# A gated linear recurrence and a maxout FFN: two time steps in each partition, and recurrence groups of one batch

## The chip, the cores and the metric

The kernel runs on one core of a Trainium2 chip. The metric is the device time of one execution in microseconds, taken as the median over runs. The profile is one further execution, recorded by the hardware profiler.

## The reference

Four inputs q, k, v and alpha have the shape (4 batches, 8 heads, 768 time steps, 48) in fp32. Each head carries a 48 by 48 state through time; the outputs of all heads, 384 values a token, go through a feed-forward network (FFN) with three parallel first layers of which the largest value is kept.

```python
for t in range(S):
    state = alpha[:, :, t, :, None] * state + einsum('bhd,bhe->bhde', k[:, :, t], v[:, :, t])
    y[:, :, t] = einsum('bhd,bhde->bhe', q[:, :, t], state)
x = y.transpose(0, 2, 1, 3).reshape(4 * 768, 384)
h = maximum(maximum(x @ w1, x @ w2), x @ w3)      # 768 wide
out = h @ w_out                                   # 3072 x 384
```

## The kernel before

**Tiles.** Time is cut into 6 blocks of 128 steps, with time on the partitions. One *unit* u is one block of one batch with all 8 heads; there are 24, block by block, with the batches inside a block. Two units are a *group* n: the same block of two batches. There are 12 groups, and a group is also what the FFN takes at a time (256 tokens).

**The recurrence, unit by unit.** `load` (L344) brings alpha, q, k and v of a group, 384 KB each in runs of 48 fp32 (192 bytes), into one of five sets of buffers. `decay` (L366) takes logarithms of alpha on ACT (L373), sums them over each half block on PE (L388, "totals") and makes from neighbouring blocks the factor G (L400). `prep` (L405) makes cumulative sums inside the block with one matmul against a triangular constant (L416), takes exponentials of them and of their negatives on ACT (L419, L421), multiplies q and k by them (L428, on POOL, or on DVE for the units listed in `EARLY`), scales v to fp16 (L439), transposes q and k on PE (L452, 16 transposes of 64 rows), copies them out of PSUM on DVE (L471), forms the scores k.q on PE (L480, 8 matmuls of 48 rows by 128 columns, of which two run on the two halves of the array's rows) and masks them on DVE (L485). `output` (L498) adds, in one PSUM bank, the part of the state (L509) and the part inside the block (L512), copies with a scale on ACT (L520), turns the result (L527) and copies it to xT on DVE (L531). `state` (L534) forms k.v over the block (L545), adds the old state on DVE (L551) and multiplies by G on POOL (L558); the state Z is kept in two copies that take turns.

**The FFN, group by group.** `ffn` (L567) has nine pieces of six matmuls (L582; three weights, two column tiles of 128, three row tiles). The piece of the first weight is copied by ACT (L590), those of the other two are joined by a maximum on DVE (L594). Then come twelve matmuls with w_out (L607), a copy on ACT (L615) and the store (L618).

**What sets the order.** Nothing is scheduled by hand: every piece of work is a step with an engine, a planned cost, a rank, what it reads and writes, and the PSUM banks it needs (eight in all). `Plan.order` runs a list schedule over all steps with these costs, and the instructions are then written out in that order, so each engine executes its own list strictly in turn. A step with `mode=1` uses half of PE's rows; the planner adds a cost for a change of mode, and from unit 6 on the scores of one unit and the transposes of the next are one step (`window`, L464). The loads and stores go through SP's queue (L350, L618), the four weights, cast to fp16 on the way, through POOL's queue (L362), each behind the k of a certain unit (`WAFTER`).

Of the kernel before, what the change touches and what calls it, by code (L numbers as in the profile page):

```python
# [18 lines left out]
CDEC = 0.92  # L19
# [4 lines left out]
TURN_RANK, TURN_COST = 2.0, 0.1  # L24
SP_FIRST = 0.9
QUEUES = ("SP", "POOL")
DMA_IN, DMA_OUT, DMA_SLOW = 0.9, 0.9, 1.0
DMA_BOTH = {"SP": 0.3, "POOL": 0.7}


class Transfers:
# [9 lines left out]
    def next(self, commit=False):  # L41
        now = self.now
        left = {e: [list(j) for j in js[:1]] for e, js in self.jobs.items()}
        while True:
# [8 lines left out]
            rate = DMA_BOTH if len(on) > 1 else dict.fromkeys(QUEUES, 1.0)  # L53
# [15 lines left out]
            return end, j[2]  # L69


class Plan:
# [55 lines left out]
    def order(self):  # L128
# [20 lines left out]
        free = dict(dict.fromkeys(HOP, 0.0), SP=SP_FIRST)  # L149
        bank_free = {b: 0.0 for b in range(NBANKS)}  # L150
        place, seq, recent = {}, [], []
# [18 lines left out]
        while len(seq) < n:  # L170
            best = None
            for e, cand in pending.items():
                pick = None
                for i in cand:
                    at = self.homes(bank_free, self.steps[i][5])
                    if at is None:
                        continue
                    t = max(ready[i], free[e], at[0])
                    turn = TURN_RANK if e == "PE" and self.steps[i][7] != mode else 0.0
                    key = (t, self.steps[i][2] + turn, i)  # L180
                    if pick is None or key < pick:
                        pick = key
                if pick is not None and (best is None or pick < best[0]):
                    best = (pick, e)
            landing = dma.next()
            if landing and (best is None or landing[0] + DMA_OUT <= best[0][0]):
                end, i = dma.next(commit=True)
                self.landed[i] = end + DMA_OUT
                finish(i, end + DMA_OUT)
                continue  # L190
# [17 lines left out]
            if load:  # L208
                dma.add(e, t + cost + DMA_IN, load, i)
            else:  # L210
                finish(i, t + cost + HOP[e])
# [7 lines left out]
def kernel(  # L219
# [38 lines left out]
    halves = np.stack([rr < HALF, rr >= HALF], axis=1).astype(np.float32)  # L258
    c16_np = np.concatenate(
        [trimid, np.eye(P), (s_ <= t_).astype(np.float32), halves], axis=1  # L260
    ).astype(np.float16)
    dec = CDEC ** (rr - (HALF - 1.0))
    c32_np = np.stack(
        [SIG / dec, dec / SIG, np.full(P, HALF * np.log(CDEC))], axis=1
# [5 lines left out]
    c16 = sb.tile([P, 3 * P + 2], FP16, name="c16")  # L270
    c32 = sb.tile([P, 3], FP32, name="c32")
    tri, ident = c16[:, :P], c16[:, P:2 * P]
    maskA, hsel = c16[:, 2 * P:3 * P], c16[:, 3 * P:]
# [9 lines left out]
    ld = {x: homes(5, [P, HG, D], FP32, x + "n") for x in "aqkv"}  # L283
    las = homes(3, [P, HG, DP], FP16, "la")
    eps = homes(3, [P, H, D], FP32, "ep")
    ens = homes(3, [P, H, D], FP32, "en")
    qks = homes(7, [P, 2, H, DP], FP16, "qk")
    v16s = homes(7, [P, H, D], FP16, "v")
    qkTs = homes(3, [P, 2, NP, P], FP16, "qkT")
    LAs = homes(3, [P, 2, NP, P], FP16, "LA")  # L290
# [4 lines left out]
    Us = homes(3, [P, NP, 2 * D], FP32, "U")  # L295
    Zs = [homes(B, [P, NP, 2 * D], FP16, f"Z{i}_") for i in range(2)]
    e12s = homes(4, [P, HG // 2, 2], FP32, "e")
    Gs = homes(3, [P, HG // 2], FP32, "G")
    wcat = sb.tile([P, NFT, 3, DF], FP16, name="wcat")
    wo16 = sb.tile([P, NJ, DM], FP16, name="wo16")  # L300
    zero = sb.tile([P, 2 * P], FP16, name="zero")
    nc.vector.memset(zero, 0.0)
    for t in las:
        nc.vector.memset(t[:, :, D:], 0.0)
    for t in qks:
        nc.vector.memset(t[:, :, :, D:], 0.0)
    for zz in Zs:
        for t in zz:
            nc.vector.memset(t, 0.0)

    plan = Plan({x: range(NBANKS) for x in ("Lp", "hp", "tp", "A", "yp", "xp", "pp", "gp", "op", "fill")})
# [13 lines left out]
    def banks2(key, dtype):  # L325
# [4 lines left out]
    LEAD = 6.5  # L330
    WAFTER = {2: (0,), 3: (1, 2), 5: (3,)}
    FILL = 0
    FUSED = 6
    pending = []
    TP = 0.24
    EARLY = {0: ("DVE", "POOL", "POOL"), 1: ("DVE", "DVE", "ACT"),
             3: ("DVE", "DVE", "ACT"), 6: ("DVE", "DVE", "POOL"),
             7: ("POOL", "POOL", "POOL")}


    views = {n: x.rearrange("b h s d -> s (b h) d") for n, x in
             (("a", alpha), ("q", q), ("k", k), ("v", v))}

    def load(n, lo, hi, names="aqkv"):  # L344
        cb, g = divmod(n, B // UB)
        for x in names:
            t = ld[x][n % 5]

            def run(x=x, t=t):
                nc.sync.dma_start(  # L350
                    t[:, lo:hi],
                    views[x][cb * P:(cb + 1) * P, g * HG + lo:g * HG + hi])

            plan.step("SP", 0.5, -1.0, run, line="loads",
                      writes=[(x, n % 5, h) for h in range(lo // H, hi // H)],
                      load=1.8 * (hi - lo) / HG)

    def weights(g, gate):
# [4 lines left out]
                  reads=[gate], writes=[("w", g)], line="weights", load=3.5)  # L363


    def decay(n):  # L366
        cb, g = divmod(n, B // UB)
        la, an = las[n % 3], ld["a"][n % 5]
        rank = 2 * n - 0.5

        def ln(lo, hi):
            plan.step("ACT", 0.11 + 0.00072 * (hi - lo) * D, rank,
                      lambda: nc.scalar.activation(out=la[:, lo:hi, :D], in_=an[:, lo:hi, :],  # L373
                                                   func=AFT.Ln, scale=1.0 / CDEC),
                      reads=[("a", n % 5, h) for h in range(lo // H, hi // H)],
                      writes=[("la", n % 3, h) for h in range(lo // H, hi // H)])

        if n == 0:
            ln(0, H)
            ln(H, HG)  # L380
        else:
            ln(0, HG)
        key = ("hp", n)

        def totals():
            live[key] = bank(key, [P, HG // 2, 2], FP32)
            for j in range(HG // 2):
                nc.tensor.matmul(live[key][:, j, :], la[:, 2 * j:2 * j + 2, :], hsel,  # L388
                                 start=True, stop=True)

        plan.step("PE", 0.2, 2 * n + 0.5, totals, banks=[key],
                  reads=[("la", n % 3, 0), ("la", n % 3, 1)], writes=[key])
        plan.step("ACT", 0.3, 2 * n + 0.5,
                  lambda: nc.scalar.activation(out=e12s[n % 4], in_=live[key], func=AFT.Exp,
                                               bias=hbias, scale=1.0),
                  reads=[key], writes=[("e", n % 4)])
        if cb > 0:
            m = n - B // UB
            plan.step("DVE", 0.1, 2 * n + 0.5,
                      lambda: nc.vector.tensor_mul(Gs[m % 3], e12s[m % 4][:, :, 1],  # L400
                                                   e12s[n % 4][:, :, 0]),
                      reads=[("e", m % 4), ("e", n % 4)], writes=[("G", m % 3)])


    def prep(u):  # L405
        n, i = divmod(u, UB)
        hs = slice(i * H, (i + 1) * H)
        la, ep, en = las[n % 3], eps[u % 3], ens[u % 3]
        qk, v16 = qks[u % 7], v16s[u % 7]
        Lk, tk = ("Lp", u), ("tp", u)  # L410
        Ak = ("A", u)
        plan.width[Ak] = 2

        def cums():
            live[Lk] = bank(Lk, [P, H, D], FP32)
            nc.tensor.matmul(live[Lk], tri, la[:, hs, :D], start=True, stop=True)  # L416

        plan.step("PE", 0.17, u, cums, banks=[Lk], reads=[("la", n % 3, i)], writes=[Lk])
# [5 lines left out]
        for w, x, e in ((0, "q", ep), (1, "k", en)):  # L424
            eng = EARLY[u][w] if u in EARLY else "POOL"
            plan.step(eng, 1.0 if eng == "POOL" else 0.5, u,
                      lambda w=w, x=x, e=e, eng=eng: (
                          nc.gpsimd if eng == "POOL" else nc.vector).tensor_mul(  # L428
                              qk[:, w, :, :D], ld[x][n % 5][:, hs], e),
                      reads=[(x, n % 5, i), ("ep" if w == 0 else "en", u % 3)],  # L430
                      writes=[("qk", u % 7, w)])
        if u in EARLY and EARLY[u][2] == "ACT":
            plan.step("ACT", 0.55, u + 0.5,
                      lambda: nc.scalar.activation(out=v16, in_=ld["v"][n % 5][:, hs],
                                                   func=AFT.Copy, scale=vsc),
                      reads=[("v", n % 5, i)], writes=[("v16", u % 7)])
        else:
            plan.step("POOL", 0.6, u,
                      lambda: nc.gpsimd.tensor_scalar(out=v16, in0=ld["v"][n % 5][:, hs],  # L439
                                                      scalar1=vsc, scalar2=1.0, op0=AOP.mult,  # L440
                                                      op1=AOP.mult),
                      reads=[("v", n % 5, i)], writes=[("v16", u % 7)])
        qkT, LA = qkTs[u % 3], LAs[u % 3]

        def trans():
            live[tk] = banks2(tk, FP16)[:, :, :2 * NP * HALF].rearrange(
                "p r (a s) -> p r a s", s=HALF)
            for w in range(2):
                for j in range(NP):
                    for r in range(2):  # L450
                        rows = slice(r * HALF, (r + 1) * HALF)
                        nc.tensor.transpose(live[tk][:, r, w * NP + j, :],  # L452
                                            qk[rows, w, 2 * j:2 * j + 2, :],
                                            ident[rows, r * HALF:(r + 1) * HALF])

        plan.width[tk] = 2
        both = u > FUSED
        flip = dict(reads=[("qk", u % 7, 0), ("qk", u % 7, 1)], writes=[tk, ("qkT room", u % 3)])
        if not both:
            plan.step("PE", TP, u, trans, banks=[tk], mode=1, **flip)  # L460
        else:
            score = pending.pop()

            def window():  # L464
                score[0]()
                trans()

# [228 lines left out]
```

## Time and profile before

| | us |
|---|---|
| median of three runs (lowest to highest) | 166.81 (166.67 to 167.28) |
| the profiled execution, its whole time | 166.16 |
| the profiled execution, span from first to last instruction | 164.4 |
| PE matmul busy | 142.0 (86%) |
| DVE busy | 117.0 (71%) |
| ACT busy | 78.0 (47%) |
| POOL busy | 71.4 (43%) |
| first FFN matmul starts | 25.03 |
| weights landed: w1, w2, w3, w_out | 24.98, 28.35, 31.76, 42.58 |

The granted TensorE clock was 0.998 of full speed. Busy times are shares of the whole span and hide stages with different limits; matmuls are pipelined and overlap, so a busy PE is not a PE at its peak. How tightly PE works is read from the distance between the starts of its matmuls: 0.109 us for an L582 in a stream of them. The weights' issues started at 16.82 us (w1, w2 and w3 behind one another) and 34.67 us (w_out).

### The profile page before, as it was taken

The numbers are of one execution on the slowest core, as the hardware profiler recorded it, in microseconds if no ns is written. First come the engines' busy times: TensorE is split into PE (matmuls) and PEld (weight loads), VectorE is DVE, ScalarE is ACT, GpSimd is POOL, SyncE is SP. The second block draws the span as 40 slices with busy tenths as digits, with TensorE's granted clock in tenths as the row PEclk, the third lists the DMA queues.
The fourth block names the chain that finished last, engine by engine and source line by source line (L and its number), as shares of the span: only waits on it lengthen the run. The fifth ranks groups of instructions, "written<-read, shape, count | busy, mean of one in ns | idle before, by whom it ended". The sixth has DMA issues, their size and how long they took to land.

```text
span 164.4 us, 4677 instructions
## 1 busy us (share of the span) xinstructions
PE 142.0 (86%) x1912; PEld 112.9 (69%) x1912; DVE 117.0 (71%) x204; ACT 78.0 (47%) x160; POOL 71.4 (43%) x103
## 2 busy tenths in 40 slices
PE   0347569999799999979998979899999999999991
PEld 0234357868568788858676868676987897878770
DVE  7186933499769998959786948972897695956360
ACT  3538185403756567275654373855424323443412
POOL 0303804090426999979877279999200000000000
PEclk9999999999999999999999999999999999999999
DMA  6999999999999999999999999966100202011112
GB/s 123 223 221 218 214 200 197 211 207 166 209 229 207 196 193 226 216 193 245 231 229 201 214 196 235 206 222 225 68 4 20 76 4 96 4 47 49 49 51 96
DMA packets 104885, 26.35 MB, mean 160 GB/s; under 512 B 99744, under 2 KB 104864, under 8 KB 104864
## 3 DMA queue, kind: packets, MB, share of 16 engines
q1 hardware_dynamic: 102592, 23.60, 70.1%
q0 software_dynamic: 1984, 2.36, 8.5%
q8 instruction: 15, 0.25, 0.7%
q10 hardware_dynamic: 288, 0.10, 0.4%
q14 instruction: 6, 0.05, 0.1%
HBM read 23.69 MB, written 4.72 MB: 173 GB/s over the span
## 4 chain that ended last, share of the span: by engine, by line
PE 45%; DMA 24%; SPq 10%; POOL 7%; DVE 6%; issue 4%; ACT 1%; ACTq 0%; DVEq 0%
PE psum L582 25%; PE psum L607 12%; SPq L350 10%; DMA kn<-in_k_dram 9%; DMA an<-in_alpha_dram 7%; DMA wo<-in_moe_w_out_dram 5%; POOL qk L428 3%; DMA vn<-in_v_dram 3%; DVE hT L594 2%; POOL Z L558 2%; PE psum L480 2%; DVE LA L485 2%; PE psum L452 1%; PE psum L509 1%; PE psum L527 1%
## 5 line engine op out<-in xcount | busy, mean ns | idle before, releaser
L582 PE MATMUL psum<-xT,wcat 128*128 128x256 f16 x648 | 80.0, 275 | 0.1
L582 PEld LDWEIGHTS <-wcat 128*128 128x128 f16 x648 | 61.0, 98 | 8.6
L594 DVE TENSOR_TENSOR hT<-psum,hT 128x512 f16<-128x512 f32 x72 | 48.8, 686 | 18.4 <-PE psum L582 14.8
L590 ACT CAST hT<-psum 128x512 f16<-128x512 f32 x36 | 21.0, 586 | 31.9 <-PE psum L582 28.1
L485 DVE TENSOR_TENSOR LA<-psum,c 128x1024 f16<-128x1024 f32 x24 | 29.0, 1216 | 5.2 <-PE psum L480 4.7
L428 POOL TENSOR_TENSOR qk<-qn,ep 128x384 f16<-128x384 f32 x20 | 20.0, 1000 | 24.5 <-ACT ep L419 12.4
L428 POOL TENSOR_TENSOR qk<-kn,en 128x384 f16<-128x384 f32 x21 | 20.9, 998 | 13.3 <-DMA kn<-in_k_dram 7.5
L607 PE MATMUL psum<-wo,hT 128*128 128x384 f16 x144 | 25.5, 326 | 0.5 <-DMA wo<-in_moe_w_out_dram 0.5
L520 ACT ACTIVATE xb<-psum,c 128x384 f16<-128x384 f32 x24 | 14.0, 584 | 11.4 <-PE psum L512 10.6
L615 ACT COPY ob<-psum 128x384 f32<-128x384 f32 x24 | 11.4, 479 | 16.8 <-PE psum L607 13.9
L607 PEld LDWEIGHTS <-hT 128*128 128x128 f16 x144 | 13.5, 98 | 8.5 <-DMA wo<-in_moe_w_out_dram 0.7
L471 DVE COPY qkT<-psum 128x1024 f16<-128x1024 f16 x24 | 16.2, 680 | 1.7 <-PE psum L452 1.7
L558 POOL TENSOR_TENSOR Z<-U,G 48x192 f16<-48x192 f32 x32 | 15.7, 505 | 2.8 <-DVE U L551 2.0
L373 ACT ACTIVATE la<-an 128x768 f16<-128x768 f32 (+1 forms) x13 | 10.3, 793 | 13.6 <-DMA an<-in_alpha_dram 13.6
L416 PE MATMUL psum<-la,c 128*128 128x384 f16 x24 | 8.7, 364 | 8.2 <-ACT la L373 8.1
L439 POOL TENSOR_SCALAR v<-vn,c 128x384 f16<-128x384 f32 x22 | 12.8, 588 | 5.9 <-DMA vn<-in_v_dram 5.4
L419 ACT ACTIVATE ep<-psum 128x384 f32<-128x384 f32 x24 | 11.9, 496 | 4.2 <-PE psum L416 3.9
L531 DVE COPY xT<-psum 128x384 f16<-128x384 f16 x24 | 8.4, 352 | 6.5 <-PE psum L527 6.4
L512 PE MATMUL psum<-v,LA 128*128 128x48 f16 x192 | 11.7, 189 | 1.0 <-DVE LA L485 0.9
L480 PE MATMUL psum<-qkT 48*128 48x128 f16 x192 | 10.4, 232 | 2.3 <-DVE qkT L471 1.4
L512 PEld LDWEIGHTS <-LA 128*128 128x128 f16 x192 | 10.0, 100 | 2.9 <-DVE LA L485 1.4
L421 ACT ACTIVATE en<-psum 128x384 f32<-128x384 f32 x24 | 11.9, 498 | 0.0
(30 smaller groups left out, 110.2 us busy)
## 6 DMA issues: line engine op xcount, KB each, us to landing
out_dram<-ob SPq DMA_DIRECT2D x24, 192.0 KB, 2.4
an<-in_alpha_dram SPq DMA_DIRECT2D x11, 384.0 KB, 6.2
qn<-in_q_dram SPq DMA_DIRECT2D x11, 384.0 KB, 6.0
kn<-in_k_dram SPq DMA_DIRECT2D x11, 384.0 KB, 5.6
vn<-in_v_dram SPq DMA_DIRECT2D x11, 384.0 KB, 5.6
wcat<-in_moe_w_dram POOLq DMA_DIRECT2D x3, 576.0 KB, 10.6
wo<-in_moe_w_out_dram POOLq DMA_DIRECT2D x1, 576.0 KB, 7.9
an<-in_alpha_dram SPq DMA_DIRECT2D x2, 192.0 KB, 3.5
```

Of the source, the lines that this page charges most:

```text
L350: nc.sync.dma_start(t[:, lo:hi], views[x][cb * P:(cb + 1) * P, g * HG + lo:g * HG + hi])
L428: nc.gpsimd if eng == "POOL" else nc.vector).tensor_mul(
L471: plan.step("DVE", 0.69, u, lambda: nc.vector.tensor_copy(out=qkT.rearrange("p w j (r s) -> p r (w j) s", r=2), in_=live[tk]), reads=[tk], ...
L480: nc.tensor.matmul(live[Ak][:, p, j * P:(j + 1) * P], qkT[rows, 1, j, :], qkT[rows, 0, j, :], start=True, stop=True)
L485: lambda: nc.vector.tensor_mul(LA.rearrange("p a b t -> p (a b) t"), live[Ak].rearrange("p a (b t) -> p (a b) t", t=P), maskA.unsqueeze(1) ...
L512: nc.tensor.matmul(yp[:, 2 * j + p, :], LA[:, p, j, :], v16[:, 2 * j + p, :], start=(cb == 0), stop=True, skip_group_check=True)
L520: lambda: nc.scalar.activation(out=xb, in_=live[yk].rearrange("p a b -> p (a b)"), func=AFT.Copy, scale=ysc),
L558: eng.tensor_mul(Zn[rows, :, cols], U[rows, :, cols], G[rows, i * NP:(i + 1) * NP].unsqueeze(2).broadcast_to([D, NP, D]))
L582: nc.tensor.matmul(live[gk][:, jj, :], wcat[:, kt, g, c0:c0 + P], xT[:, kt, :], start=(kt == 0), stop=(kt == NFT - 1))
L590: plan.step("ACT", 0.59, r, lambda h=h, gk=gk: nc.scalar.copy(out=h, in_=live[gk]), reads=[gk], writes=[("hT", n % 3, j)])
L594: lambda h=h, gk=gk: nc.vector.tensor_max(h, live[gk], h),
L607: nc.tensor.matmul(live[ok], hT[:, kt, i * P:(i + 1) * P], wo16[:, kt, :], start=(kt == 0), stop=(kt == NJ - 1))
```

## The change

**Two neighbouring steps in a partition.** A partition now holds the time steps 2p and 2p+1 of 256, so a load moves runs of 96 fp32 (384 bytes). A group is two neighbouring blocks of one batch (256 steps, 8 heads): partitions 0 to 63 are its first block, 64 to 127 its second. A unit is now half the heads (4) of a group. There are still 12 groups and 24 units.

**The recurrence for these tiles.** The logarithm is taken in two instructions, one for each of the two steps. Cumulative sums are four matmuls of 192 columns against block-diagonal triangular constants, in place of one of 384. Transposes still take 64 rows, now one block each. Scores are 16 matmuls of 48 rows by 64 columns (two head halves by two blocks). State sums and the part inside the block are matmuls of 64 rows, in pairs. The state passes through both blocks of a group: Zs[0] is the state ahead of the first, Zs[1] that ahead of the second, with a factor G0 inside the group and G1 between groups, and `carry` in place of `decayed`. The two output banks of a group are held from the state's part until both halves of the heads are added. xT is written with every second element, which restores the order of time.

**Order.** The planner's DMA model and constants differ, half-array steps on PE are held until there is enough of them, `window` is gone, the weights' gates and `EARLY` are new, and the clearing of Z moves from DVE to POOL. The FFN's arithmetic is unchanged. In the new numbering its lines are L644 and L668; the recurrence has L399 (totals), L446 (cumulative sums), L486 (transposes), L506 (scores), L538 (state sums), L574 and L596 (outputs), L618 (turn), L622 (xT), L460 (q, k), L472 (v).

By the order of PE's instructions: 2,448 matmuls in place of 1,912, and 74 changes between steps of the whole array and steps of half of its rows in place of 50.

```diff
-    views = {n: x.rearrange("b h s d -> s (b h) d") for n, x in
+    views = {n: x.rearrange("b h (c q r) d -> b c q h (r d)", q=P, r=2) for n, x in
              (("a", alpha), ("q", q), ("k", k), ("v", v))}
...
-    WAFTER = {2: (0,), 3: (1, 2), 5: (3,)}
-    EARLY = {0: ("DVE", "POOL", "POOL"), 1: ("DVE", "DVE", "ACT"),
-             3: ("DVE", "DVE", "ACT"), 6: ("DVE", "DVE", "POOL"),
-             7: ("POOL", "POOL", "POOL")}
+    WAFTER = {4: (0,), 6: (1,), 9: (2,), 11: (3,)}
+    EARLY = {1: ("POOL", "DVE", "POOL"), 2: ("DVE", "POOL", "POOL"),
+             4: ("POOL", "POOL", "POOL"), 7: ("DVE", "POOL", "POOL")}
...
         def cums():
-            live[Lk] = bank(Lk, [P, H, D], FP32)
-            nc.tensor.matmul(live[Lk], tri, la[:, hs, :D], start=True, stop=True)
+            live[Lk] = bank(Lk, [P, HH, 2, D], FP32)
+            for rt in range(2):
+                for rs in range(2):
+                    nc.tensor.matmul(live[Lk][:, :, rt, :], tri[rt][rs], la[:, rs, hs, :D],
+                                     start=(rs == 0), stop=(rs == 1))
...
         def scores():
             live[Ak] = banks2(Ak, FP32)
-            for j in range(NP):
-                for p in range(2):
-                    rows = slice(p * DP, p * DP + D)
-                    nc.tensor.matmul(live[Ak][:, p, j * P:(j + 1) * P],
-                                     qkT[rows, 1, j, :], qkT[rows, 0, j, :], start=True, stop=True)
+            for j in range(2):
+                for r in range(2):
+                    for i in range(UB):
+                        for p in range(2):
+                            rows = slice(p * DP, p * DP + D)
+                            at = (2 * j + r) * P
+                            nc.tensor.matmul(
+                                live[Ak][i * HALF:(i + 1) * HALF, p, at:at + P],
+                                qkT[rows, i, 1, j, r * HALF:(r + 1) * HALF],
+                                qkT[rows, i, 0, j, :], start=True, stop=True)
...
+        def intra(hh):
...
+            for j in range(2):
+                for p in range(2):
+                    for r in range(2):
+                        for i in range(UB):
+                            rows = slice(i * HALF, (i + 1) * HALF)
+                            h = 4 * hh + 2 * j + p
+                            nc.tensor.matmul(live[keys[i]][:, h, :], LA[rows, p, j, r, :],
+                                             v16[rows, 2 * j + p, r, :],
+                                             start=(h == 0 and r == 0 and not old[i]),
+                                             stop=(r == 1), skip_group_check=True)
...
-                  lambda: nc.vector.tensor_copy(out=xTs[n][:, :, i * P:(i + 1) * P], in_=live[xk]),
+                      lambda i=i, xk=xk: nc.vector.tensor_copy(
+                          out=xTs[n][:, :, i * P:(i + 1) * P].rearrange(
+                              "f a (q r) -> f a r q", r=2),
+                          in_=live[xk].rearrange("f a (r q) -> f a r q", r=2)),
```

## The prediction

> **What bounds the kernel now.** First the 40 slices of the page, to see which engine is full when.
>
> ```profile
> PE   0347569999799999979998979899999999999991
> DMA  6999999999999999999999999966100202011112
> GB/s 123 223 221 218 214 200 197 211 207 166 209 229 207 196 193 226 216 193 245 231 229 201 214 196 235 206 222 225 68 4 20 76 4 96 4 47 49 49 51 96
> ```
>
> DMA is full until slice 28 (about 113 us), PE from slice 7 (25 us) on. The chain in order of time tells which of the two ends the run:
>
> ```profile
> 17.23 15.47 DMA kn<-in_k_dram
> ...
> 119.61 0.33 PE psum L480 x8
> 119.94 0.23 PE psum L452 x16
> 120.17 2.73 PE psum L582 x24
> ...
> 124.76 1.95 PE psum L607 x12
> ...
> 146.99 5.89 PE psum L582 x54
> 152.88 1.95 PE psum L607 x12
> 154.83 3.93 PE psum L582 x36
> 158.76 1.64 PE psum L607 x10
> 160.47 0.28 ACT ob L615
> ```
>
> The end is PE without gaps, and it gives PE's prices: L582 5.89/54 = 0.109 us, L607 1.95/12 = 0.1625. Sixteen transposes (L452) take 0.23. After them 24 L582 take 2.73 and not 2.62: leaving the half-array form (64 rows) costs 0.1 us. By the starts of the matmuls L582 to L480 is 0.205 instead of 0.109, so entering costs as much (I take 0.095 each); L480 to L452, both 64 rows by 128 columns, costs nothing. Without its 0.1 a block of 8 scores is 0.22 us. From the chain also: one cumulative sum (L416) 0.16, totals 0.2 a group, outputs (L509, L512) 0.37, turn (L527) 0.17, state sums (L545) 0.17 for 4.
>
> PE's own work is then 648 x 0.109 + 144 x 0.1625 = 94.0 for the FFN and 24 x (0.16 + 0.23 + 0.22 + 0.17) + 12 x 0.2 + 20 x (0.37 + 0.17) + 4 x 0.21 + 50 changes of form x 0.095 = 37.5: 131.5 us. The first matmul starts at 4.6, the last at 160.4, so PE stood for 24.4 us: 14.7 before the first L582 at 25.03, 9.7 behind it. The stages:
>
> ```profile
> core 0: us, PE busy (x) PEld busy (x) DVE busy (x) ACT busy (x) POOL busy (x), PEclk, DMA share, GB/s
> 88.00:96.00 8.00, 6.91 (x95) 5.52 (x93) 6.12 (x10) 3.75 (x8) 3.90 (x8) 1.00 1.11 214
> 112.00:120.00 8.00, 8.00 (x123) 6.39 (x119) 5.36 (x9) 3.09 (x6) 4.01 (x7) 1.00 0.33 116
> 120.00:128.00 8.00, 8.00 (x115) 6.64 (x108) 6.53 (x10) 3.20 (x6) 0.00 (x0) 1.00 0.08 27
> ```
>
> While loads run, PE has holes (1.1 us in the first row); once they are in, 0.2 us in 47. The waits name the cause:
>
> ```profile
> ACT la L373 <- DMA an<-in_alpha_dram: 13.6, 9, 3.6
> POOL qk L428 <- DMA kn<-in_k_dram: 7.5, 4, 5.3
> POOL qk L428 <- DMA qn<-in_q_dram: 5.5, 1, 5.5
> ```
>
> Of the 9.7 us, four holes of PE (by the starts of its matmuls 0.55 at 41.5, 1.2 at 72, 0.93 at 89.2, 1.23 at 96.8) go back to the first of these, twice directly and twice because xb stands behind the waiting la on ACT: 3.9 us. So the loads look like the bound and are worth at most 3.9 us behind 25.03; ahead of it they are worth what they bring the first L582 forward. The run is start + PE's work + holes: 25.03 + 125.7 (131.5 less the 5.8 done by then) + 9.7 + 4.0 behind the last matmul's start = 164.4.
>
> **The loads.** Runs of 192 bytes become 384. The trace's packet records have 15 ns for 192 bytes and 66 for the 1,536 of an output; on that line 384 take 22, and half as many packets need 0.74 of the time. A 384 KB load lands each 1.80 us now (12.13, 13.93, 15.75, 17.55), then each 1.34, an estimate; the ends are 0.9 (cost by packet) and 1.80 (by byte). The first lands at 4.0 still (the constants grow from 96 to 230 KB ahead of it), group 0 is in at 8.7 (10.3 before), k of group 1 at 12.7 (15.75).
>
> **The first FFN block.** L582 started at 25.03 because w1 landed at 24.98, 8.16 us behind its issue at 16.82; no gain in loads passes that by. In the new order POOL does, from k of group 1 on, k (1.0), q (1.0), v (0.59), k (1.0), then the issue: 12.7 + 3.6 = 16.3. The first FFN block starts at 16.3 + 8.2 = 24.5: 0.5 us gained, not 3, since POOL takes alone what DVE and POOL shared. The other weights leave at about 17.8, 21.5 and 24; PE reaches the first use of each some 2, 3 and 4 us behind its landing (the order has 30, 60 and 90 FFN matmuls ahead of them), so they hold nothing. While weights stream, loads creep, as between 20 and 29 us now (21 KB/us against 215); but group 2 is in at 19.4, so it is not caught as k was (15.47 us in the chain).
>
> **PE's work added.** Cumulative sums: one matmul of 384 columns becomes four of 192: 4 x 0.0825 = 0.33 for 0.16, 24 times: +4.0. Transposes and totals: same count and columns, 0. State sums: 128 in pairs on two row halves, 64 x 0.042, and 32 of one half alone, 32 x 0.042: 4.0 for 3.4, +0.7. Outputs inside a step: 384 of 64 rows for 192 of 128, in pairs at about 0.027: 5.2 for 5.0, +0.2. Changes between whole and half array: 74 for 50 in the order, +2.3. Scores: 16 of 64x64 for 8 of 64x128. If four tiles run at once, as two do now (pairs each 0.056), 0.23 for 0.22: 0; if two, 0.45: +5.3. I take 0, the row being pairs that do overlap, and keep the other.
>
> The scores bring a third form, 64 by 64, and the order has 33 steps between it and 64 by 128. No row shows that change: L480 to L452 (64 rows, same columns) costs 0, L582 to L480 (the form changes) 0.095. I take 0.095, since here the form changes: +3.1, with 0 as the low end. The Trainium skill, TensorEngine Tiling (Key Properties), says that changing the tiling mode, not just the tile, drains the engine; by that rule the term is 3.1, and reading it as for rows only makes it 0. The trace agrees for whole against half.
>
> In all +10.3, or 7.2 without the last term. By the new order 8.9 us of PE's work (sums and scores of five steps) lie ahead of the first FFN matmul, against 5.8 now, in time when PE stands anyway. Behind it are 131.5 + 10.3 - 8.9 = 132.9 us, against 125.7.
>
> **The other engines.** ACT: Ln in two, 2 x 0.52 for 0.84, +0.2 a group; it is 47% busy: 0. POOL: 45 q/k products at 1.0, 24 v at 0.59, 32 Z at 0.5 and the issues are 79 us for 71; 6.6 a group where PE needs 11: 0, once the start is past. DVE: ten more G at 0.35 (+3.5), four fewer q/k products (-2.6), memsets to POOL (-1.7), and xT now written every second element: 0.352 each, or up to 0.55 if the stride costs it the quicker rate that 0.680 for 1,024 fp16 shows against 1.216 at L485: 0 to +4.8. DVE has 116 to 121 us for 117, 84 to 88% between 25 and 145 us, against 76% in the stretch without holes (112 to 144); PE hides it while an FFN block is ready, and pays in holes when not.
>
> **Holes behind the first FFN block.** 9.7 less the 3.9 of loads is 5.8. The other end is the rate of the last 47 us (0.2) over 120 us, and 1.2 for PE's slow first matmuls (0.21 each until 27.1): 1.7. I take 4.4, nearer the upper end: DVE is fuller than in those 47 us, and each group of outputs now holds two PSUM banks through four steps.
>
> **Sum.** 24.5 + 132.9 + 4.4 + 4.0 = 165.8, against 164.4: +1.4. The profiled execution took 166.16 (1.8 around the span) and the median is 0.65 above it: 166.81 + 1.4 = 168.2.
>
> **Rivals.** (1) Faster: changes within the half array are free (-3.1) and holes fall to 1.7 (-2.7): 162.4. For it: the 47 us without holes. Against it: DVE. It decides from the point where both together are below 6.1 us (7.5 in my sum). 0.33. (2) The scores' tiles run two at a time: +5.3, 173.5. No row has a 64-column tile, for or against. The same page (Restrictions) says column tiling disables fast weight load, which would act this way; no run here shows it. 0.12. (3) The terms cancel, within 0.5%: 166.8, 0.14. (4) Longer runs bring nothing: 1.8 us a load. k of group 1 lands at 15.75 as now, the first FFN block moves to 27.5 and the 3.9 of holes stay: 168.2 + 3.0 + 3.9 = 175.1. Against it: 66 ns for 1,536 bytes. 0.04. My forecast has 0.37.
>
> **Numbers.** A measurement here tells about 0.5% (0.8 us) from no change. Slower is forecast, (2) and (4): 0.53; same 0.14; faster 0.33. The range is 162.0 to 174.0: it takes in (1) and (2). The forecast's own is 167 to 171 (holes 3.2 to 7).
>
> **What would show it.** Right: loads landing each 1.3 to 1.4 us and DMA done by 90 to 100 us; the first FFN matmul at 24 to 25.5; four L446 at 0.33; 16 L506 at about 0.23 with some 0.1 more on each side; PE without long waits on DMA from 25 us on, and still later at the end. Wrong: the first FFN matmul before 23 us, PE's work below 138 us, or L506 at 0.4 and more.

## The result, and the profile after

The changed kernel took 171.07 us (median of 4 runs, 170.54 to 171.68) against 166.74 for the kernel before (4 runs beside them): ratio 1.0257, 95% interval 1.0204 to 1.0310. The forecast was 168.2, slower, in a range of 162.0 to 174.0. So the way was right, and the step of 4.3 us is three times the 1.4 that was forecast. Runs that took over 1.5% more than the fastest of the same kernel, one of 250.01 us among them, are left out of the ratios here and below. The profiled execution took 170.56 us, its span is 168.8, the granted clock 1.0.

The 40 slices of the changed kernel's page, for PE, the DMA engines and the bytes they moved:

```profile
PE   0477867999999999999999999999999999998991
DMA  6999999999999999999799301102011002020202
GB/s 136 264 261 264 262 206 227 205 250 244 270 266 239 270 263 283 281 280 266 175 282 292 118 4 49 50 2 97 4 49 48 0 4 93 4 93 0 97 0 93
```

The last load lands at 93.5 us and not at 109.3; the bytes moved are 261 to 264 GB/s early on where they were 214 to 223. PE has no hole in its row between the first FFN block and the last slices. It stands less, and yet the end is later. The chain in order of time (start, us, what) shows the longer list and its prices:

```profile
28.30 2.36 PE psum L644 x12
...
37.19 0.35 PE psum L506 x16
37.54 0.31 PE psum L596 x16
37.84 1.42 PE psum L644 x12
39.26 0.33 PE psum L446 x4
...
115.31 0.35 PE psum L506 x16
115.65 1.42 PE psum L644 x12
...
157.27 5.89 PE psum L644 x54
163.16 1.64 PE psum L668 x10
```

Four cumulative sums take 0.33, as forecast. Sixteen scores with the change that follows take 0.35, so about 0.255 without it, and the 16 output matmuls behind them (0.31) end with another. An FFN matmul still costs 5.89/54 = 0.109. The stages, with the columns of the table shown of before:

```profile
88.00:96.00 8.00, 7.67 (x143) 6.08 (x141) 5.63 (x9) 4.53 (x11) 5.91 (x9) 1.00 0.81 239
112.00:120.00 8.00, 8.00 (x160) 6.20 (x156) 6.48 (x12) 3.53 (x8) 4.08 (x6) 1.00 0.15 52
```

The hole of 1.1 us between 88 and 96 us is 0.33 now. From 112 to 120 us PE was full before and is full now, but it starts 160 matmuls where it started 123: the stage is filled with smaller ones. Of the waits on loads, one large one is left (us in total, times, longest), and all of it lies ahead of 20 us:

```profile
ACT la L384 <- DMA an<-in_alpha_dram: 7.3, 3, 3.7
```

Put into the prediction's sum (start of the first FFN matmul, PE's work behind it counted from its list at the same prices, holes behind it, 4.0 from the last matmul's start; it closes to 0.2 us):

| | first FFN matmul | work behind it | holes behind it | span |
|---|---|---|---|---|
| before | 25.0 | 125.8 | 9.8 | 164.4 |
| forecast | 24.5 | 132.9 | 4.4 | 165.8 |
| after | 28.2 | 132.9 | 3.9 | 168.8 |

The work is a count and not a measurement: it agrees with the forecast because the list and the prices are the same. What the trace measures is the time from the first FFN matmul's start to that of the last matmul, 136.6 us (135.4 before), and the holes are what the count leaves of it. Work and holes together came out as forecast within 0.5 us. The start is 3.7 us late, more than the 3.0 by which the span was missed. The timeline of the changed kernel ahead of that first matmul (start, us, engine, instruction, in brackets the wait):

```profile
23.62 0.33 DVE L427 TENSOR_TENSOR Z<-psum,G 48x192 f16<-48x192 f32 x1
...
23.88 1.73 DVE L410 TENSOR_TENSOR G<-e 128x4 f32<-128x4 f32 x1
24.57 1.01 POOL L460 TENSOR_TENSOR qk<-kn,en 128x384 f16<-128x384 f32 x1
25.62 0.36 DVE L427 TENSOR_TENSOR Z<-psum,G 48x192 f16<-48x192 f32 x1
...
26.04 0.50 PE L574 MATMUL psum<-Z,qkT 128*128 128x96 f16 x4 [2.18 <-DVE Z L427]
...
28.23 0.61 PE L644 MATMUL psum<-xT,wcat 128*128 128x256 f16 x2
```

PE's list puts the outputs L574 of the next group ahead of the first FFN matmul. They wait for the second half of Z, and that stands on DVE behind one G of 128x4, which took 1.73 us and ended at 25.61, 0.03 us behind the end of POOL's product (25.58). All G of this line (lowest, median and highest ns):

```profile
L410 DVE TENSOR_TENSOR G<-e x12: 146/168/1725, 8.2 to 132.6; 128x4 f32<-128x4 f32 x12
```

Eight of the twelve take 0.15 to 0.20 us. w1 had landed at 25.79, 2.4 us ahead of the first FFN matmul. The wait for Z (2.18 us) is most of that; PE's own list from L574 to the first L644 takes another 2.2 us, which could have run before w1 landed.

### The profile page after: what moved, and what is told of

Its sections match the earlier page's. It is cut to its first block, busy times and chain, and to the rows that moved or that the text cites. A ratio compares the mean times of both kernels' runs of the same rounds, so it can differ in the third digit from the quotient of the medians.

```text
span 168.8 us, 5790 instructions
## 1 busy us (share of the span) xinstructions
PE 152.2 (90%) x2448; PEld 121.1 (72%) x2448; DVE 121.2 (72%) x200; ACT 77.9 (46%) x171; POOL 80.3 (48%) x117
## 4 chain that ended last, share of the span: by engine, by line
PE 82%; DVE 3%; ACT 1%; issue 1%; ACTq 0%
PE psum L644 44%; PE psum L668 14%; PE psum L446 4%; PE psum L506 4%; PE psum L596 4%; PE psum L486 3%; PE psum L618 3%; PE psum L538 2%; PE psum L574 2%; PE psum L399 1%; DVE G L410 1%; DVE LA L515 1%; ACT xb L610 1%; DVE Z L427 0%; DVE qkT L494 0%
## 5 line engine op out<-in xcount | busy, mean ns | idle before, releaser
L644 PE MATMUL psum<-xT,wcat 128*128 128x256 f16 x648 | 82.2, 275 | 0.0
L644 PEld LDWEIGHTS <-wcat 128*128 128x128 f16 x648 | 60.5, 98 | 8.3
L460 POOL TENSOR_TENSOR qk<-qn,ep 128x384 f16<-128x384 f32 x22 | 22.0, 998 | 23.6 <-ACT ep L451 22.3
L668 PE MATMUL psum<-wo,hT 128*128 128x384 f16 x144 | 26.4, 326 | 0.0
L460 POOL TENSOR_TENSOR qk<-kn,en 128x384 f16<-128x384 f32 x23 | 23.3, 1013 | 3.3 <-ACT ep L451 2.9
L446 PE MATMUL psum<-la,c 128*128 128x192 f16 x96 | 14.0, 272 | 5.4 <-ACT la L384 5.3
L668 PEld LDWEIGHTS <-hT 128*128 128x128 f16 x144 | 13.5, 98 | 7.4
L494 DVE COPY qkT<-psum 128x1024 f16<-128x1024 f16 x24 | 16.3, 685 | 2.9 <-PE psum L486 2.8
L451 ACT ACTIVATE ep<-psum 128x384 f32<-128x384 f32 x24 | 11.9, 497 | 13.9 <-PE psum L446 13.6
L622 DVE COPY xT<-psum 128x384 f16<-128x384 f16 x24 | 13.3, 581 | 5.0 <-PE psum L618 4.9
L472 POOL TENSOR_SCALAR v<-vn,c 128x384 f16<-128x384 f32 x24 | 14.1, 593 | 5.1 <-PE psum L596 3.9
L384 ACT ACTIVATE la<-an 128x384 f16<-128x384 f32 (+1 forms) x26 | 12.0, 503 | 7.5 <-DMA an<-in_alpha_dram 7.3
L427 POOL TENSOR_TENSOR Z<-U,G 48x192 f16<-48x192 f32 x16 | 8.1, 504 | 14.5 <-DVE U L551 13.9
L427 POOL TENSOR_TENSOR Z<-V,H 48x192 f16<-48x192 f32 x16 | 8.1, 503 | 13.3 <-DVE H L415 12.5
L446 PEld LDWEIGHTS <-c 128*128 128x128 f16 x96 | 8.9, 104 | 6.3 <-DMA c<-const 3.9
L506 PE MATMUL psum<-qkT 48*64 48x128 f16 x384 | 11.1, 240 | 1.3 <-DVE qkT L494 1.3
L486 PE MATMUL psum<-c,qk 64*128 64x64 f16 x384 | 10.6, 200 | 1.4 <-POOL qk L460 1.3
```

The costliest lines, as they stand in the source:

```text
L427: (nc.gpsimd if eng == "POOL" else nc.vector).tensor_mul(Zn[rows, :, cols], src[rows, :, cols], G[rows].unsqueeze(2).broadcast_to([D, NP, D]))
L446: nc.tensor.matmul(live[Lk][:, :, rt, :], tri[rt][rs], la[:, rs, hs, :D], start=(rs == 0), stop=(rs == 1))
L486: nc.tensor.transpose(live[tk][:, i, at:at + HALF], qk[rows, w, r, 2 * j:2 * j + 2, :], ident[rows, rows])
L494: lambda: nc.vector.tensor_copy(out=qkT.rearrange("p i w j t -> p i (w j t)"), in_=live[tk]),
L506: nc.tensor.matmul(live[Ak][i * HALF:(i + 1) * HALF, p, at:at + P], qkT[rows, i, 1, j, r * HALF:(r + 1) * HALF], qkT[rows, i, 0, j, :], st ...
L644: nc.tensor.matmul(live[gk][:, jj, :], wcat[:, kt, g, c0:c0 + P], xT[:, kt, :], start=(kt == 0), stop=(kt == NFT - 1))
```

## The experiments

My theory after this comparison: the loads give back holes, PE's added work takes more than that, and the start slipped for two reasons, slower loads than I took (1.3 us) and G behind POOL (up to 2.4 us). Rivals: DVE as the bound, scores in pairs, and a start set by the weights alone. The first four kernels ran beside the kernel before at 167.19 us (19 runs). In each, work behind the start is counted as above, and the holes are what it leaves.

**The longer runs alone, in the kernel before.** The loads move 384-byte runs into the same buffers; the values land in other places, everything else is the kernel before.

```diff
-    views = {n: x.rearrange("b h s d -> s (b h) d") for n, x in
+    views = {n: x.rearrange("b h (c q r) d -> b c q h (r d)", q=P, r=2) for n, x in
...
-                    t[:, lo:hi],
-                    views[x][cb * P:(cb + 1) * P, g * HG + lo:g * HG + hi])
+                    t[:, lo:hi].rearrange("p (h r) d -> p h (r d)", r=2),
+                    views[x][n % 4, n // 4][:, lo // 2:hi // 2])
```

> The kernel before with one thing changed: its loads move runs of 384 bytes, as after the change. The values come from other places of the same inputs, so the output is not the reference's; every instruction list is that of before. Theory (the change's gain is the loads, its loss is PE's added work): a 384 KB load each 1.50 us instead of 1.80, k of group 1 lands some 1.3 us sooner and w1 with it, and the 3.9 us of holes that go back to loads close: about 161.5 us, 5.2 less than 166.7. Rival (the loads are hidden anyway): within 0.5 us of 166.7. Rival (the loads bound the kernel): a gain near the 17% of load time, over 10 us.

Measured: 163.29 us, ratio 0.9784 (0.9751 to 0.9817), span 161.7. Holes behind the first FFN matmul fall from 9.8 to 7.1; that matmul starts at 24.98, where it was. Its waits:

```profile
ACT la L373 <- DMA an<-in_alpha_dram: 3.5, 4, 1.2
...
PE psum L582 <- DMA wcat<-in_moe_w_dram: 2.7, 1, 2.7
```

The wait of la on alpha falls from 13.6 us to 3.5. But w1, issued at 16.04 and not 16.82, landed 8.9 us later where it took 8.16: while it streams, the loads go on beside it, and between its issue and its landing they now move 1.13 MB and not 0.76. So faster loads are worth 2.2% to this kernel, all of it from holes, and nothing at the start; my theory had w1 sooner and all 3.9 us of holes closed, and its 161.5 us were 1.8 too low. The prediction's "at most 3.9 us" behind the start stands as an upper bound for this order; the measured part is 2.7.

**The shorter runs, in the changed kernel.** The same exchange the other way round.

```diff
-                nc.sync.dma_start(t[:, lo:hi].rearrange("p h r d -> p h (r d)"),
-                                  views[x][b, c][:, lo:hi])
+                cb, g = divmod(n, 2)
+                nc.sync.dma_start(
+                    t[:, lo:hi].rearrange("p h r d -> p (h r) d"),
+                    views[x][cb * P:(cb + 1) * P, 16 * g + 2 * lo:16 * g + 2 * hi])
```

> The changed kernel with only its loads taken back to runs of 192 bytes (the values come from other places of the inputs, so the output is not the reference's). Theory: loads 1.80 us again, w1 lands 1.3 us later, and group 2's k may be caught behind the weights as it was before; the first FFN matmul moves from 28.2 to between 29.5 and 35, and up to 3.9 us of holes come back: 173 to 181 us against 171.1. Rival (the loads are hidden anyway): 171.

Measured: 185.91 us, ratio 1.1125 (1.1077 to 1.1172), more than was expected. From its chain in order of time:

```profile
20.46 16.13 DMA vn<-in_v_dram
...
84.23 6.89 DMA an<-in_alpha_dram
```

One v of group 2 is caught behind the weights for 16 us, as k was in the kernel before, and behind the first FFN matmul (29.65) 19.7 us are left beside the counted work. They are not holes alone: where PE stood, the granted clock was lower, 0.77 between 32 and 40 us (PE busy for 3.7 of 8) and 0.68 between 88 and 96 (3.6 of 8), and in the full stretches behind these it was still 0.80 and 0.89. The new order is built for loads of this speed: in it the runs are worth 8.7% of the kernel before's time (1.1125 less 1.0257), in the old one 2.2%.

**Scores without the third form.** The 16 score matmuls become 8 of 64-row tiles by 128 columns, as before the change; their products land in the wrong places, so this is a kernel for its time alone.

```diff
-                for r in range(2):
-                    for i in range(UB):
-                        for p in range(2):
...
-                            at = (2 * j + r) * P
-                            nc.tensor.matmul(
-                                live[Ak][i * HALF:(i + 1) * HALF, p, at:at + P],
-                                qkT[rows, i, 1, j, r * HALF:(r + 1) * HALF],
-                                qkT[rows, i, 0, j, :], start=True, stop=True)
+                for i in range(UB):
+                    for p in range(2):
+                        rows = slice(p * DP, p * DP + D)
+                        at = (2 * j + i) * P
+                        nc.tensor.matmul(live[Ak][:, p, at:at + P], qkT[rows, i, 1, j, :],
+                                         qkT[rows, i, 0, j, :], start=True, stop=True)
```

> The changed kernel with the scores as 8 matmuls of 64 by 128 tiles instead of 16 of 64 by 64; the products land in other places than they should, the rest is untouched. Theory (a change between the two half-array forms drains PE for 0.095 us): 33 changes fewer, -3.1, and 0.01 to 0.02 us a block less, in all -3.0 to -3.5: about 168 us. Rival (such changes are free): -0.5 at most, 170.6. Rival (64-column tiles run two at a time): -5 or more.

Measured: 167.52 us, ratio 1.0014 (0.9982 to 1.0046), span 165.8. Changes of form fall from 107 to 74 and the work behind the start to 130.0; the start falls to 26.54, because G took 0.14 us in this run; holes are 5.4. Of the 3.0 us of span 1.7 are the start, 2.9 the work, and 1.5 come back as holes. So the time is where my theory had it, but more than half of the gain is the start, for another reason. What shows the price of the change is the distance between the last score and the first output matmul behind it: 0.148 us in the changed kernel and 0.052 here, where the form stays. From its chain:

```profile
44.01 0.23 PE psum L505 x8
49.79 0.33 PE psum L505 x8
```

Eight scores take 0.23 between half-array steps and 0.33 with a change. Sixteen of 64 by 64 take 0.255, which is the price of four at a time and not of two (0.45): the scores themselves cost next to nothing, the form does.

**Two of four cumulative sums.** The matmuls that bring one step of a pair into the other are left out.

```diff
-                for rs in range(2):
-                    nc.tensor.matmul(live[Lk][:, :, rt, :], tri[rt][rs], la[:, rs, hs, :D],
-                                     start=(rs == 0), stop=(rs == 1))
+                nc.tensor.matmul(live[Lk][:, :, rt, :], tri[rt][rt], la[:, rt, hs, :D],
+                                 start=True, stop=True)
```

> The changed kernel without two of the four matmuls of each cumulative sum (those across the two steps of a partition); the rest is untouched. Theory (behind the first FFN matmul PE's work passes into the time one for one): 20 to 24 times 0.165, -3.3 to -4.0: about 167.4 us. Rival (DVE, fuller by xT and G, holds the rest): -0.5 at most, 170.6.

Measured: 167.77 us, ratio 1.0047 (1.0008 to 1.0085), span 165.6. Work behind the start 129.9 (3.0 less), start 27.08, holes 4.8. Of the 3.0 us, 2.1 come off the time behind the first FFN matmul and 0.9 come back as holes; the other 1.1 of the span are the start (the G ahead of it took 0.57 us and not 1.73). So PE's work does not pass into the time one for one, though my theory had it so, and the time of 167.8 came near its 167.4 by help of the start.

**Both at once.** The two edits above together.

> The changed kernel without two of the four matmuls of each cumulative sum and with the scores as 8 matmuls of 64 rows by 128 columns (both leave out or misplace part of the recurrence's sums); the longer runs of the loads, the strided xT and the rest stay. Alone the first took 0.0210 off the ratio and the second 0.0243. My theory: what the change adds on PE is what makes it slower, and the two are PE's time and add up: work behind the first FFN matmul 132.9 - 3.0 - 2.9 = 127.0, start at 26.5 to 27.1, holes 5 to 6, sum about 163, ratio 0.98 to 0.985, where the kernel before with the long runs alone stands too (0.978). Rival: with PE's list shorter DVE (121 us in the changed kernel against 117 before) becomes the bound: holes rise by what the work falls in the second edit, ratio 0.995 to 1.0.

This kernel and the next three ran beside a kernel before that took 168.42 us (13 runs, 166.96 to 169.27), up to 1% longer than elsewhere; why is not known. Their ratios are against that, and against 166.74 each would be 1% higher; I compare them with the changed kernel by the spans and terms of the profiles. Measured: ratio 0.9866 (0.9783 to 0.9948), span 163.3; start 25.97, work behind it 127.0, holes 6.4. From its chain, then from its waits:

```profile
35.51 0.33 PE psum L504 x8
...
37.46 0.17 PE psum L445 x2
```

```profile
ACT la L384 <- DMA an<-in_alpha_dram: 13.5, 9, 2.9
```

The span is 1.1 us below the kernel before: without 5.9 us of PE's work, by the count, the change wins. Against the changed kernel it is 5.5 us shorter. Of these 2.3 are the start, where the G on Z's way took 0.29 us and ended earlier, and 3.3 are the time behind it; with the changed kernel's start it would, by this sum, still be 1.1 us slower than before. The ratio is just above the expected 0.98 to 0.985, whose bounds its interval takes in, and below the rival's 0.995 to 1.0. The 2.5 us that come back as holes are, by the waits, those of loads again: behind the first FFN matmul la waits 6.2 us for alpha (five times, the last until 73.5), which it never does there in the changed kernel, and PE's longest distance between matmuls, 1.1 us, ends at 75.4 with a wait for an en of ACT. The start stands at w1's landing (25.93).

**G on POOL.** One edit (and the same at L415): the small product leaves DVE.

```diff
-                  lambda: nc.vector.tensor_mul(G0s[n % 2], e[:, :, 0, 1], e[:, :, 1, 0]),
+                  lambda: nc.gpsimd.tensor_mul(G0s[n % 2], e[:, :, 0, 1], e[:, :, 1, 0]),
```

> The changed kernel with one edit: the factors G (L410, L415; 128x4) are multiplied on POOL and not on DVE; PE's and ACT's lists are the same. My theory: ahead of the first FFN matmul PE waited 2.18 us for Z, Z stood on DVE behind a G that took 1.73 us (23.88 to 25.61) while POOL ran a product of k (24.57 to 25.58). On POOL the G runs between two products, Z comes when the state sums are in, and the first FFN matmul starts at 26 to 26.8 and not at 28.2; w1 lands at 25.8 and bounds it below. PE's work behind it (132.9) and its holes (3.9) stay: ratio to the kernel before about 1.014, 169.3 us. Rival: the weights (25.8) and PE's own list ahead set the start, so that G only hid another wait: start at 28, no gain, 1.025. A third: G waits on POOL behind the products queued ahead of it as long as it waited on DVE; then too no gain, and Z (L427) shows the wait.

Measured: 169.83 us (169.54 to 170.62), ratio 1.0116 (1.0042 to 1.0191), span 167.9. Start 26.86, work 132.9, holes 4.3. The group of G (lowest, median and highest ns), then the timeline ahead of the first FFN matmul:

```profile
L410 POOL TENSOR_TENSOR G<-e x12: 195/202/207, 8.9 to 129.7; 128x4 f32<-128x4 f32 x12
```

```profile
23.84 0.70 DVE L427 TENSOR_TENSOR Z<-psum,G 48x192 f16<-48x192 f32 x2
...
24.59 0.50 PE L574 MATMUL psum<-Z,qkT 128*128 128x96 f16 x4 [0.54 <-DVE Z L427]
...
26.86 2.10 PE L644 MATMUL psum<-xT,wcat 128*128 128x256 f16 x9
```

All twelve G take 0.2 us, the two halves of Z follow each other, and the start moves by 1.4 us, to the late end of what was expected (26 to 26.8); 0.5 come back as holes. By the profiles the gain is 0.9 us. The weights alone did not set the start, since they landed at 25.80.

**G on POOL, and w1 sooner.** w1 leaves behind the k of unit 1; the planner reorders around it.

```diff
-    WAFTER = {4: (0,), 6: (1,), 9: (2,), 11: (3,)}
+    WAFTER = {3: (0,), 6: (1,), 9: (2,), 11: (3,)}
```

> As the kernel with G on POOL, and w1 leaves behind the k of unit 1, at about 13 us, and not behind the v16 of unit 2, at 18.0; the planner then puts the first 12 FFN matmuls behind the state sums of group 0 and one set of cumulative sums. If the landing of w1 sets the start (8 us behind the issue, as 17.96 to 25.79), the first FFN matmul starts at 21 to 22. PE's work ahead of it is less (some 8 us instead of 9), so work behind it is about 133.8; the loads of group 1 share the queues with w1 and come 3 to 4 us later, which costs 1 to 4 us in holes more than the 3.9. Sum 21.5 + 133.8 + 6.5 + 4.0 = 165.8, with 1.8 around it about 167.5 to 168: ratio 1.00 to 1.01. Rival: the first FFN matmuls come early but PE then stands for the late loads, so that what the start wins comes back whole as holes: 1.014, as the kernel with G on POOL alone.

Measured: ratio 1.0108 (0.9996 to 1.0219) from two of its four runs (168.92 and 170.89 us), span 168.7. The rival fits better: by the span nothing is won. From its timeline, then from its chain:

```profile
23.21 2.13 PE L644 MATMUL psum<-xT,wcat 128*128 128x256 f16 x12
```

```profile
29.06 38.87 DMA an<-in_alpha_dram x5
```

The first FFN matmul starts at 23.2, 3.7 us sooner than with G on POOL alone, but 3.6 us behind w1's landing (19.59): the landing does not set this start, though my theory had it so. The work behind it grows by 0.9 and the holes by 3.6 (to 7.9). The chain now runs through alpha's loads up to 68 us, and la waits 8.7 us for alpha behind the first FFN matmul, where it does not with G on POOL alone. That w1's early transfer is what delays these loads is my reading; no run separates it from the new order.

**xT in plain order.** xT is copied without the stride, so that the tokens come out in another order.

```diff
-                          out=xTs[n][:, :, i * P:(i + 1) * P].rearrange(
-                              "f a (q r) -> f a r q", r=2),
-                          in_=live[xk].rearrange("f a (r q) -> f a r q", r=2)),
+                          out=xTs[n][:, :, i * P:(i + 1) * P], in_=live[xk]),
```

> The changed kernel with xT (L622) written in plain order, not to every second element (the tokens then stand in another order in the output). 24 copies should fall from 0.58 us to about 0.35: 5.5 us of DVE. My theory: PE is the bound behind the first FFN matmul (holes 3.9 in all), so DVE's time is hidden: ratio 1.020 to 1.026, at most 0.6 us won where PE waits for the first xT. Rival: DVE's 121 us is what makes the holes and the start late: -3 us or more, 1.007 or below.

Measured: 169.71 us (10 runs, 168.84 to 171.09), ratio 1.0098 (1.0058 to 1.0137), below my theory's range and above the rival's. Span 167.7: start 26.41, work 132.9, holes 4.6. The group of xT in the changed kernel and here, then G in the timeline ahead of the first FFN matmul:

```profile
L622 DVE COPY xT<-psum x24: 564/582/598, 21.4 to 156.3; 128x384 f16<-128x384 f16 x24
L622 DVE COPY xT<-psum x24: 341/348/359, 21.3 to 155.2; 128x384 f16<-128x384 f16 x24
```

```profile
23.63 0.15 DVE L410 TENSOR_TENSOR G<-e 128x4 f32<-128x4 f32 x1
```

The copies fall from 0.58 us to 0.35, which is 5.6 us of DVE. Behind the start nothing of that arrives: work is the same and the holes are 0.7 higher (la waits for alpha again, until 75.1, and PE's longest distance between matmuls until then, 0.56 us, ends at 76.9). What the span won (1.1) is the start, 1.8 us sooner: G came 0.25 us sooner than in the changed kernel, ahead of POOL's issue of w3, and took 0.15. So DVE's time is hidden, as I took it, and whether G meets POOL hangs on tenths of a microsecond.

## Why the prediction was right, and where it was not

**Right: the sign; its size was not.** It held that the loads only look like the bound and that what they give back is less than what PE's list takes. The longer runs alone give 2.2%; the work they need on PE costs 7.1 us behind the start (132.9 for 125.8), against 5.9 us of holes won. But that is a loss of 1.2 us. The other 3.2 of the 4.4 by which the span grew are the start, which the prediction had as a gain of 0.5. So the mechanism named explains about a quarter of the loss. Had the start come as forecast, the sum would be 0.7 us above that of before, less than the 0.8 that the prediction could tell from no change: the sign held in part by luck, since a term that was wrong pushed the same way. The median, 171.07, lies just outside the forecast's own 167 to 171 and inside the wide range; of its signs of being right, the pace of the loads (1.3 to 1.4) and the start (24 to 25.5) did not come.

**Right: the prices of PE's work.** Cumulative sums 0.33 (forecast 0.33); half of them taken out is 3.0 us by the count, of which 2.1 arrived. The scores 0.255 a block (forecast 0.23; the rival of two at a time 0.45). The unmeasured change between 64x64 and 64x128 was taken at 0.095: by the starts of the matmuls L506 to L596 and L506 to L486 are 0.148 us, where the same two kinds of steps without a change of form (L480 to L452, before) are 0.053: 0.095. With the scores in 64x128 form the first of these falls to 0.052. The Trainium skill, TensorEngine Tiling (Key Properties), has a drain at each change of tiling mode; the trace agrees, with 0.095 us each, also where only the columns change. The faster rival rested on this change being free, and falls with it.

**Right in number: holes 4.4 (3.9).** The reasons given for taking 4.4 and not less, a fuller DVE and the output banks held longer, are not shown. xT's stride costs 0.23 us a copy, just above what was allowed (0.58 against at most 0.55), and without it the holes are not fewer. PE's two longest distances behind the start, 0.53 us at 92.7 and 0.91 at 154.8, end with a wait for xb on ACT. The 5.9 us of holes won are also 2 more than the 3.9 that loads were to be worth; the runs do not separate that part from the new order and PE's longer list.

**Wrong: the first FFN matmul, 24.5 forecast, 28.2 measured.** Two terms of that step:
- "then each 1.34, an estimate": loads land each 1.50 us (11.39, 12.91, 14.41, 15.91). The estimate drew a line through 192 and 1,536 bytes; the changed kernel's packets of 384 bytes take 24 ns (median), not 22, against 15 for 192, and half as many of these are 0.80 of the time, not 0.74. So k of group 1 came at 14.41 and not 12.7, w1 left at 17.96 and not 16.3, and landed at 25.79 and not 24.5; the 3.6 us from k to the issue held (3.55), and the 8.2 to the landing was 7.8. Group 2 was in at 22.8 and not 19.4; alpha of group 3 was then caught behind the weights (issued at 18.31, landed at 33.40), but nobody waited for it. The rival by which longer runs bring nothing falls with 1.50 for 1.80. The Trainium skill, DMA: Bandwidth & Descriptors (Why small descriptors are slow), gives a fixed cost of some 3 cycles a packet beside 32 bytes a cycle; as an estimate from these figures, half as many packets of twice the size take 15/18 = 0.83 of the time, and the trace agrees (1.50/1.80 = 0.83).
- The step named w1 as the only thing the start waits for. It left out PE's list ahead of the FFN and what each entry waits for: L574, Z, G, and G behind POOL. That cost 2.4 us in the profiled execution; taking G off DVE gave 1.4 of it back, a G that came ahead of POOL's issue 1.8 (xT in plain order), and in the kernel with both edits the first FFN matmul started when w1 landed (25.97, 25.93).

With both in place the sum is 25.8 + 132.9 + 4.4 + 4.0 = 167.1 for the weights alone and 2.4 more with G, which is 169.5 against 168.8 measured; the holes (3.9) and the 0.2 by which the sum closes are the rest.

**Open.** G entered DVE at 23.88 and POOL's product at 24.57; in the 0.69 us between, POOL was issuing w3 (23.75 to 24.55). In the kernel with 8 scores a G that began 0.05 us behind the start of the same issue took 0.14. Why the first waited through the issue, and did not end ahead of the product, is not settled.

## What to carry to other kernels

Price a layout that speeds up loads by what it makes the busiest engine do, at the measured cost of one instruction and of each change between tile forms, before counting what the loads win: here 384-byte runs are worth 2.2% by themselves, and the sums they need cost 7.1 us where 5.9 us of holes are won. Do not expect all of the work that PE is spared to come off the end: of 3.0 us 2.1 did, and of 5.9 us 3.3, since the loads then hold PE again. For the start of a pipeline, walk the list of the engine that starts it, entry by entry, down to the smallest instruction on the engines that feed it; a transfer's landing is only one of the candidates. When an early start is bought by moving a transfer forward, look at which transfers it shares the queues with, for the time may come back as holes.

## What was not expected of the hardware

- **A small DVE instruction waits for POOL's whole one.** Of the G products of L410 on DVE (L412 in the kernel with runs of 192 bytes), with both operands in SBUF, each that took over 0.25 us (up to 1.73) ended 0.01 to 0.03 us behind the end of an instruction of POOL, in the changed kernel and in five of the others; the rest took 0.14 to 0.23. The Trainium skill, SBUF — State Buffer (SBUF: two separate sides), describes a port pair that DVE and GpSimd lock for a whole instruction, whichever starts first, among others by a DVE instruction with two SBUF inputs against a POOL instruction that reads SBUF; the trace agrees, but for the longest one (1.73 us), which had started 0.69 us ahead of the product that it waited for (see Open).
- **The granted clock fell where PE stood in the middle of a run.** In the changed kernel with runs of 192 bytes the clock was 0.77 and 0.68 in the two stretches of 8 us in which PE was busy for less than half, and 0.80 and 0.89 in the full ones behind them; it is part of why the same exchange of 192 for 384 bytes is 2.2% in one order and 8.7% in the other.
- **A DVE copy of 128x384 fp16 out of PSUM that writes every second element** is slower by two thirds: 0.58 us for 0.35.
